# Grouped-query attention with a cache: six heads of the output weight moved to a second DMA queue, ring of eight slots instead of nine

## The chip, the cores and the metric

One core of a Trainium2 chip runs the program. The metric is the device time of one execution in microseconds (us). The kernel before was run three times: 388.24, 388.26 and 388.43 us, median 388.26 us.

The core has five instruction streams: PE (TensorE), DVE (VectorE), ACT (ScalarE), POOL (GpSimd) and SP (SyncE), and sixteen DMA engines that move data between device memory and the on-chip memory. In this kernel POOL and SP issue the transfers.

## The reference

```python
B, Sq, D = 32, 4, 1024
Hq, Hkv, Sk, Dh = 32, 4, 2048, 128
q = (x @ wq).reshape(B, Sq, Hq, Dh).transpose(0, 2, 1, 3)
k = jnp.repeat(k_cache, Hq // Hkv, axis=1)
v = jnp.repeat(v_cache, Hq // Hkv, axis=1)
scores = jnp.einsum("bhqd,bhkd->bhqk", q, k) * (Dh ** -0.5)
p = softmax(scores, axis=-1)
o = jnp.einsum("bhqk,bhkd->bhqd", p, v)
out = o.transpose(0, 2, 1, 3).reshape(B, Sq, Hq * Dh) @ wo
```

All inputs are bf16. For each of 32 batches the kernel reads 2 MB of keys and 2 MB of values; `wq` and `wo` are 8 MB each. That is about 151 MB in all, each byte used once.

## The kernel before

**The ring.** `slots` is a buffer of nine slots (`NSLOT`) of 8192 bf16 elements per partition, 2 MB each. All large inputs go through it in the order of the list `stream`: four loads of `wq`, then k of batches 0, 1 and 2, then v(0), k(3), v(1), k(4) and so on to k(31), v(29), v(30), v(31), and at last four loads of `wo`. Entry n uses slot n mod `NSLOT`. Each entry is four transfers of 512 KB with a semaphore for each; POOL issues them all, in order, at L144. Before entry n POOL waits until the work that reads entry n - `NSLOT` is done (`freed`): the last transposes of a k, the product `pv` of a v, the query projection for `wq`. For k and v a transfer is one group of heads; for `wo` it is a piece of two heads, two rows of 2 KB in each of 128 partitions. SP loads `x` at the start (L146) and stores the output at the end (L168); between these it has nothing to do.

**The work of a batch.** k arrives with positions on the partitions and is transposed on TensorE (`kt_fill`, L236, eight fills per batch into a ring of four PSUM banks), evacuated by DVE and ACT (L346, L348) into `KT_sb`. `qk` (L281) makes the scores of a batch in one PSUM tile; DVE takes the maximum (L372), ACT the exponential with its sum (L401), DVE the reciprocal and a diagonal matrix of it (L381, L382). `tr_fill` (L252) transposes the probabilities and scales them by that diagonal; `pv` (L263) multiplies with v; `ot_evac` (L361) copies the result into `oT_sb`. TensorE's order is written out: for batch i it runs `qk(i)`, `pv(i-1)`, the eight fills of k(i+2), and the four `tr_fill` of batch i.

**The output projection.** After `pv(31)` TensorE runs `oproj` (L314): 32 heads times two halves of 512 columns, 64 matmuls that accumulate in one PSUM tile, all of them reading `oT_sb` with the columns of all batches. They are queued in sixteen groups of four, each with a wait for its piece of `wo`. DVE and ACT then evacuate one half each (L391, L411), and SP stores the output.

`Program.emit` (L48) turns the named events into semaphore waits on each engine; an engine runs its list in order.

Of the kernel before, what the change touches and what calls it, by code (L numbers as in the profile page):

```python
# [8 lines left out]
BF16 = mybir.dt.bfloat16  # L9
# [45 lines left out]
def bass_standalone__gqa_block_cached__sampling_kernel(  # L55
# [8 lines left out]
    B, Sq, D = x.shape  # L64
    _, Hkv, Sk, Dh = k_cache.shape
    Hq = wq.shape[1] // Dh
# [5 lines left out]
    NKT = Sk // 128  # L72
    G = Hkv
    scale = float(Dh) ** -0.5
    NSLOT = 9
    SLOT = 8192
    NRING = 4
    KT_FILLS = 2 * G
    TR_FILLS = 4
    AHEAD = 2  # L80
    WQ_LOADS = 4
    WO_LOADS = 4
    HPL = Hq // WO_LOADS
    WO_PARTS = 4
    WO_PER = HPL // WO_PARTS

    x_flat = x.rearrange("b s d -> (b s) d")
    out_flat = out.rearrange("b s d -> (b s) d")
# [1 line left out]
    pr = Program()  # L90

    with ExitStack() as es:
        sb = lambda name, shape, dt: es.enter_context(nc.sbuf_tensor(name, shape, dt))
        slots = sb("slots", [128, NSLOT, SLOT], BF16)
        KT_sb = sb("KT_sb", [128, 2, G, Sk], BF16)
        QT_sb = sb("QT_sb", [128, B, Hq, Sq], BF16)
        oT_sb = sb("oT_sb", [128, Hq, NT], BF16)
# [18 lines left out]
        q_bank = ring_f32 + [ps_s[:, c * 512:(c + 1) * 512] for c in range(4)]  # L116

        pr.sems = {e: es.enter_context(nc.semaphore(f"s_{e}")) for e in Program.ENGINES}
        for n in ["x", "out"] + [f"slot{i}_{g}" for i in range(NSLOT) for g in range(G)] + [f"wo{i}" for i in range(WO_LOADS * WO_PARTS)]:
            pr.sems[n] = es.enter_context(nc.semaphore(f"s_{n}"))  # L120


# [3 lines left out]
        for b in range(B):  # L126
            stream.append(("v", b))
            if b + AHEAD + 1 < B:
                stream.append(("k", b + AHEAD + 1))
        stream += [("wo", i) for i in range(WO_LOADS)]  # L130
        slot_of = {l: n % NSLOT for n, l in enumerate(stream)}

        def freed(l):
            kind, i = l
            return {"wq": ("qproj", i), "k": ("kt", i, KT_FILLS - 1), "v": ("pv", i)}[kind]

        def slot(l):
            return slots[:, slot_of[l], :]

        wq_v = wq.rearrange("(p a k) n -> p a (k n)", a=WQ_LOADS, k=KT // WQ_LOADS)  # L140
        wo_v = wo.rearrange("(h p) n -> p h n", p=128)

        def fetch(dst, src):
            return lambda e: e.dma_start(dst, src, single_packet=True)  # L144
# [4 lines left out]
            out=ident[:], in_=ident[:], compare_op=ALU.not_equal, fill=1.0, base=0,  # L149
            pattern=[[-1, 128]], channel_multiplier=1), ["zero"], "ident")  # L150
        for n, l in enumerate(stream):
            kind, i = l
            waits = [freed(stream[n - NSLOT])] if n >= NSLOT else []
            s, v = f"slot{n % NSLOT}_", 16 * (n // NSLOT + 1)
            if kind == "wq":
                for q in range(G):
                    cols = slice(q * SLOT // G, (q + 1) * SLOT // G)
                    pr.load("pool", fetch(slot(l)[:, cols], wq_v[:, i, cols]), l + (q,), s + str(q), v, waits)
            elif kind in "kv":
                src = (k_cache if kind == "k" else v_cache)[i].rearrange("g (p t) d -> g p (t d)", p=128)  # L160
                for g in range(G):
                    pr.load("pool", fetch(slot(l)[:, g * NKT * Dh:(g + 1) * NKT * Dh], src[g]), l + (g,), s + str(g), v, waits)
            else:
                for q in range(WO_PARTS):
                    part = slot(l)[:, q * WO_PER * D:(q + 1) * WO_PER * D].rearrange("p (h n) -> p h n", n=D)
                    h0 = i * HPL + q * WO_PER
                    pr.load("pool", fetch(part, wo_v[:, h0:h0 + WO_PER, :]), ("wo", i, q), f"wo{i * WO_PARTS + q}", 16, waits)
        pr.op("sp", lambda e: e.dma_start(out_flat[:, :], out_sb).then_inc(pr.sems["out"], 16), ["out0", "out1"])  # L168
        pr.op("sp", lambda e: e.wait_ge(pr.sems["out"], 16))

# [135 lines left out]
                tr_fill(i, f)  # L306
        pv(B - 1)

        def oproj(i, h0, n):
            def fn(e):  # L310
                w = slot(("wo", i)).rearrange("p (h n) -> p h n", n=D)
                for h in range(h0, h0 + n):
                    for c in range(2):
                        ins = e.matmul(  # L314
                            ps_s[:, c * 512:(c + 1) * 512],
                            lhsT=oT_sb[:, h, :],
                            rhs=w[:, h - i * HPL, c * 512:(c + 1) * 512],
                            start=(h == 0),
                            stop=(h == Hq - 1),
                        )  # L320
                return ins

            return fn

        for i in range(WO_LOADS):
            for q in range(WO_PARTS):
                pr.op("pe", oproj(i, i * HPL + q * WO_PER, WO_PER),
                      [("wo", i, q), ("ot", B - 1), ("exp", B - 1)],
                      "oproj" if (i, q) == (WO_LOADS - 1, WO_PARTS - 1) else None)


        def evac(job):
# [131 lines left out]
```

## Time and profile before

| | |
|---|---|
| median of three runs | 388.26 us (388.24 to 388.43) |
| profiled execution: span | 386.1 us |
| profiled execution: its own time | not recorded beside the span; the median lies 2.2 us above the span |
| moved by DMA | 152.30 MB, mean 394 GB/s over the span |
| busy share of PE, DVE, ACT, POOL | 76%, 64%, 51%, 40% |
| k and v transfers, issue to landing (median) | 41.4 and 42.2 us |
| x transfer, issue to landing | 2.6 us |
| output transfer, issue to landing | 2.0 us |

How to read it: the span goes from the first to the last instruction of one profiled execution. The queue table names the queues: q0 is the ring (issued by POOL), q1 is SP's queue, q8 and q14 fetch the engines' instructions. DMA share is the mean busy share of the sixteen DMA engines in a stretch; the GB/s are what they moved in it. In the timeline a line gives start, length, engine, line of the kernel, operation, the tiles written and read, and in brackets the idle time before it and what ended that. PEclk is the part of TensorE's full clock that was granted. The chain of work that ended last goes back from the last instruction, at each step to what released it. The trace also records when each transfer raised its semaphore; it does so sixteen times, and the last of these is its landing.

### The profile page before, as it was taken

What the parts mean: (1) busy time and instruction counts of PE and PEld (TensorE: products, weight loads), DVE (VectorE), ACT (ScalarE), POOL (GpSimd) and SP (SyncE); (2) the same over time, 40 slices, a digit from 0 to 9 for tenths busy, and PEclk for the clock granted to TensorE, in tenths of its full rate; (3) what the DMA queues carried; (4) which work ended last, traced back from release to release, by engine and by line L of the source; (5) the groups of instructions that cost most, each with busy time, mean ns of one, the idle gap of its engine ahead of it and who ended that gap; (6) DMA issues with size and microseconds to landing.
All of it is one profiled execution on the core that took longest, in us unless ns stands there. A gap on an engine that the chain in (4) does not pass through costs nothing.

```text
span 386.1 us, 12016 instructions
## 1 busy us (share of the span) xinstructions
PE 293.4 (76%) x5446; PEld 238.9 (62%) x5448; DVE 245.3 (64%) x390; ACT 198.6 (51%) x230; POOL 154.1 (40%) x294
## 2 busy tenths in 40 slices
PE   1969777878887877677978877787868778776596
PEld 0968556666766666465866766666756666664542
DVE  0017887777676777677677777686767766774400
ACT  1016666655564666456656455466564666654300
POOL 8975344433344443344443334443334436500000
PEclk9999999999898999999899899898989999997689
DMA  7999999999999999999999999999999999999982
GB/s 276 413 407 407 407 407 407 409 408 407 407 410 407 409 408 407 405 409 406 408 409 404 410 407 410 407 411 407 406 408 408 409 408 406 410 407 404 389 322 112
DMA packets 41810, 152.30 MB, mean 394 GB/s; under 512 B 4640, under 2 KB 4640, under 8 KB 41760
## 3 DMA queue, kind: packets, MB, share of 16 engines
q0 software_dynamic: 41472, 151.01, 98.5%
q8 instruction: 43, 0.70, 0.8%
q1 hardware_dynamic: 288, 0.52, 0.5%
q14 instruction: 7, 0.06, 0.0%
HBM read 151.26 MB, written 0.26 MB: 392 GB/s over the span
## 4 chain that ended last, share of the span: by engine, by line
DMA 83%; PE 7%; POOL 5%; ACT 2%; issue 1%; POOLq 0%; DVE 0%
DMA slots<-in_k_cache_dram 45%; DMA slots<-in_v_cache_dram 23%; DMA slots<-in_wo_dram 11%; POOL slots L144 5%; DMA slots<-in_wq_dram 4%; ACT KT_sb L348 2%; PE ps_o L263 2%; PE ps_c L236 1%; PE ps_o L236 1%; PE ps_a L236 1%; PE ps_s L281 1%; PE ps_s L211 0%; PE ps_b L236 0%; PE ps_s L314 0%; PE ps_o L252 0%
## 5 line engine op out<-in xcount | busy, mean ns | idle before, releaser
L401 ACT ACTIVATE pp_sb<-ps_s,negmx 128x2048 bf16<-128x2048 f32 x32 | 62.9, 1967 | 93.0 <-DVE negmx L373 93.0
L144 POOL DMA_DIRECT2D slots<-in_k_cache_dram x128 | 66.8, 529 | 100.1 <-PE ps_o L263 93.1
L372 DVE TENSOR_REDUCE mx<-ps_s 128x1 f32<-128x2048 f32 x32 | 73.3, 2291 | 38.6 <-PE ps_s L281 38.6
L144 POOL DMA_DIRECT2D slots<-in_v_cache_dram x128 | 66.9, 529 | 75.3 <-PE ps_a L252 66.0
L263 PEld LDWEIGHTS ps_o<-pp_sb,slots 128*128 128x128 bf16 x2048 | 54.4, 97 | 53.6 <-issue 53.6
L263 PE MATMUL ps_o<-pp_sb,slots 128*128 128x32 bf16 x2048 | 56.9, 179 | 38.6 <-DMA slots<-in_v_cache_dram 37.6
L348 ACT ACTIVATE KT_sb<-ps_a 128x1024 bf16<-128x1024 bf16 x32 | 32.7, 1022 | 34.8 <-PE ps_a L236 34.7
L236 PE MATMUL ps_c<-ident,slots 128*128 128x128 bf16 x512 | 40.9, 224 | 7.5 <-DMA slots<-in_k_cache_dram 5.5
L346 DVE COPY KT_sb<-ps_b 128x1024 bf16<-128x1024 bf16 x64 | 43.6, 682 | 1.2 <-PE ps_b L236 0.8
L236 PE MATMUL ps_a<-ident,slots 128*128 128x128 bf16 x512 | 42.1, 229 | 2.0 <-DVE KT_sb L346 1.4
L236 PE MATMUL ps_b<-ident,slots 128*128 128x128 bf16 x512 | 41.8, 228 | 0.0
L236 PE MATMUL ps_o<-ident,slots 128*128 128x128 bf16 x512 | 40.2, 222 | 2.0 <-DVE KT_sb L346 1.0
L236 PEld LDWEIGHTS ps_c<-ident,slots 128*128 128x128 bf16 x512 | 31.7, 101 | 11.1 <-DMA slots<-in_k_cache_dram 9.8
L348 ACT ACTIVATE KT_sb<-ps_c 128x1024 bf16<-128x1024 bf16 x32 | 32.7, 1022 | 8.4 <-PE ps_c L236 8.4
L236 PEld LDWEIGHTS ps_a<-ident,slots 128*128 128x128 bf16 x512 | 31.7, 102 | 6.0 <-DMA slots<-in_k_cache_dram 3.0
L236 PEld LDWEIGHTS ps_o<-ident,slots 128*128 128x128 bf16 x512 | 31.7, 99 | 4.4 <-DVE KT_sb L346 3.1
L281 PE MATMUL ps_s<-KT_sb,QT_sb 128*32 128x512 bf16 x512 | 34.3, 389 | 0.0
L236 PEld LDWEIGHTS ps_b<-ident,slots 128*128 128x128 bf16 x512 | 33.9, 103 | 0.1
L346 DVE CAST pp_sb<-ps_a 128x512 bf16<-128x512 f32 x32 | 22.1, 691 | 17.9 <-PE ps_a L252 17.9
L348 ACT ACTIVATE KT_sb<-ps_o 128x1024 bf16<-128x1024 bf16 x32 | 32.7, 1022 | 0.2 <-PE ps_o L236 0.2
L346 DVE COPY KT_sb<-ps_a 128x1024 bf16<-128x1024 bf16 x32 | 22.1, 690 | 7.9 <-PE ps_a L236 7.9
L252 PE MATMUL ps_o<-diag,pp_sb 128*128 128x128 bf16 x128 | 13.2, 227 | 15.3 <-ACT KT_sb L348 15.3
(50 smaller groups left out, 308.9 us busy)
## 6 DMA issues: line engine op xcount, KB each, us to landing
slots<-in_k_cache_dram POOLq DMA_DIRECT2D x128, 512.0 KB, 41.4
slots<-in_v_cache_dram POOLq DMA_DIRECT2D x128, 512.0 KB, 42.2
slots<-in_wq_dram POOLq DMA_DIRECT2D x16, 512.0 KB, 9.8
slots<-in_wo_dram POOLq DMA_DIRECT2D x16, 512.0 KB, 42.6
pp_sb<-in_x_dram SPq DMA_DIRECT2D x1, 256.0 KB, 2.6
out_dram<-pp_sb SPq DMA_DIRECT2D x1, 256.0 KB, 2.0
```

What stands on the lines that cost most here:

```text
L144: return lambda e: e.dma_start(dst, src, single_packet=True)
L236: ins = e.transpose(dst[:, q * 128:(q + 1) * 128], slot(("k", b))[:, (g * NKT + t) * Dh:(g * NKT + t + 1) * Dh], ident[:, :],)
L252: ins = e.matmul(dst[:, q * 128:(q + 1) * 128], lhsT=P_sb[:, t * 128:(t + 1) * 128], rhs=diag[:, b % 2, :], start=True, stop=True)
L263: ins = e.matmul(ps_o[:, 32 * g:32 * (g + 1)], lhsT=v[:, (g * NKT + t) * Dh:(g * NKT + t + 1) * Dh], rhs=PT_sb[:, t, 32 * g:32 * (g + 1)], ...
L281: ins = e.matmul(ps_s[32 * g:32 * (g + 1), c * 512:(c + 1) * 512], lhsT=QT_sb[:, i, REP * g:REP * (g + 1), :], rhs=KT_sb[:, i % 2, g, c * ...
L346: pr.op("dve", lambda e: e.tensor_copy(dst, src), w, ("evac",) + job)
L348: pr.op("act", lambda e: e.activation(dst, src, ACT.Copy), w, ("evac",) + job)
L372: pr.op("dve", lambda e, i=i: e.tensor_reduce(mx[:, i:i + 1], ps_s[:, :], AX.X, ALU.max), [("qk", i)], ("max", i))
L401: pr.op("act", lambda e, i=i: e.activation(P_sb, ps_s[:, :], ACT.Exp, bias=negmx[:, i:i + 1], scale=scale, accum_out=ssum[:, i:i + 1]), [( ...
```

## The change

Six of the 32 heads of `wo` (`HSIDE`, 1.5 MB) leave the ring. They get a buffer of their own, `side` (12 KB per partition), and SP loads them right after `x` in sixteen transfers, without a wait. Transfer m takes eight partitions, four apart (m = 0: partitions 0, 4, ... 28), and in each the six rows of 2 KB. All sixteen raise one semaphore, `side`; the projection waits for its full count of 256.

The ring has eight slots instead of nine. `wo` is in it with 26 heads, that is thirteen pieces of two heads: three loads of four pieces and one load of one.

The projection starts with the six heads of `side` in one group of twelve matmuls, then goes through the thirteen pieces. Number and order of the matmuls stay as they were, by heads from 0 to 31.

```diff
-    NSLOT = 9
+    NSLOT = 8
...
-    WO_LOADS = 4
-    HPL = Hq // WO_LOADS
+    HSIDE = 6
+    WO_PER = 2
     WO_PARTS = 4
-    WO_PER = HPL // WO_PARTS
+    HPL = WO_PER * WO_PARTS
+    WO_PIECES = (Hq - HSIDE) // WO_PER
+    WO_LOADS = -(-WO_PIECES // WO_PARTS)
...
+        side = sb("side", [128, HSIDE, D], BF16)
...
-                for q in range(WO_PARTS):
+                for q in range(min(WO_PARTS, WO_PIECES - i * WO_PARTS)):
                     part = slot(l)[:, q * WO_PER * D:(q + 1) * WO_PER * D].rearrange("p (h n) -> p h n", n=D)
-                    h0 = i * HPL + q * WO_PER
+                    h0 = HSIDE + i * HPL + q * WO_PER
                     pr.load("pool", fetch(part, wo_v[:, h0:h0 + WO_PER, :]), ("wo", i, q), f"wo{i * WO_PARTS + q}", 16, waits)
+        for m in range(16):
+            p0 = 32 * (m // 4) + m % 4
+            pr.load("sp", lambda e, p0=p0: e.dma_start(side[p0:p0 + 29:4, :, :], wo_v[p0:p0 + 29:4, 0:HSIDE, :]),
+                    ("side", m), "side", 16 * 16)
...
-        for i in range(WO_LOADS):
-            for q in range(WO_PARTS):
-                pr.op("pe", oproj(i, i * HPL + q * WO_PER, WO_PER),
-                      [("wo", i, q), ("ot", B - 1), ("exp", B - 1)],
-                      "oproj" if (i, q) == (WO_LOADS - 1, WO_PARTS - 1) else None)
+        pr.op("pe", oproj(side, 0, HSIDE), [("side", 15), ("ot", B - 1), ("exp", B - 1)])
+        for n in range(WO_PIECES):
+            i, q = divmod(n, WO_PARTS)
+            w = slot(("wo", i))[:, q * WO_PER * D:(q + 1) * WO_PER * D].rearrange("p (h n) -> p h n", n=D)
+            pr.op("pe", oproj(w, HSIDE + n * WO_PER, WO_PER), [("wo", i, q)], "oproj" if n == WO_PIECES - 1 else None)
```

More of the change, by code (lines that the diff above doesn't have):

```diff
@@ L118, in bass_standalone__gqa_block_cached__sampling_kernel @@
         pr.sems = {e: es.enter_context(nc.semaphore(f"s_{e}")) for e in Program.ENGINES}
-        for n in ["x", "out"] + [f"slot{i}_{g}" for i in range(NSLOT) for g in range(G)] + [f"wo{i}" for i in range(WO_LOADS * WO_PARTS)]:
+        for n in ["x", "out"] + [f"slot{i}_{g}" for i in range(NSLOT) for g in range(G)] + [f"wo{i}" for i in range(WO_PIECES)] + ["side"]:
             pr.sems[n] = es.enter_context(nc.semaphore(f"s_{n}"))
@@ L307, in bass_standalone__gqa_block_cached__sampling_kernel, with oproj @@
         pv(B - 1)
-        def oproj(i, h0, n):
+        def oproj(w, h0, n):
             def fn(e):
-                w = slot(("wo", i)).rearrange("p (h n) -> p h n", n=D)
                 for h in range(h0, h0 + n):
@@ L316, in fn @@
                             lhsT=oT_sb[:, h, :],
-                            rhs=w[:, h - i * HPL, c * 512:(c + 1) * 512],
+                            rhs=w[:, h - h0, c * 512:(c + 1) * 512],
                             start=(h == 0),
```

## The prediction

> **What bounds the kernel now.** I read the page first: the queue table and the chain of work that ended last.
>
> ```profile
> q0 software_dynamic: 41472, 151.01, 98.5%
> q8 instruction: 43, 0.70, 0.8%
> q1 hardware_dynamic: 288, 0.52, 0.5%
> q14 instruction: 7, 0.06, 0.0%
> ...
> DMA 83%; PE 7%; POOL 5%; ACT 2%; issue 1%; POOLq 0%; DVE 0%
> ```
>
> The ring's transfers (q0) fill 98.5% of the sixteen DMA engines' time, and 83% of the chain is transfers. The change moves bytes from q0 to q1 and adds none, so the average says "no change". The end must therefore be read by itself. Here is the windows view (length, busy of PE, PEld, DVE, ACT, POOL, granted clock, DMA share, GB/s) at the start and in the last stage:
>
> ```profile
> 2.00:3.00 1.00, 0.00 (x0) 0.00 (x0) 0.00 (x0) 0.03 (x1) 1.00 (x3) 1.00 0.74 227
> 3.00:4.00 1.00, 0.61 (x6) 0.61 (x7) 0.00 (x0) 0.00 (x0) 1.00 (x3) 1.00 0.69 115
> 4.00:5.00 1.00, 0.46 (x5) 0.21 (x2) 0.50 (x1) 0.00 (x0) 1.00 (x3) 1.00 0.98 360
> ...
> 370.00:372.00 2.00, 2.00 (x11) 0.94 (x10) 0.00 (x0) 0.00 (x0) 0.00 (x0) 1.00 1.04 389
> 372.00:374.00 2.00, 2.00 (x11) 0.90 (x10) 0.00 (x0) 0.00 (x0) 0.00 (x0) 1.00 0.72 279
> 374.00:376.00 2.00, 2.00 (x11) 0.88 (x9) 0.00 (x0) 0.00 (x0) 0.00 (x0) 1.00 0.55 219
> 376.00:378.00 2.00, 2.00 (x11) 0.92 (x10) 0.00 (x0) 0.00 (x0) 0.00 (x0) 1.00 0.52 205
> 378.00:380.00 2.00, 1.95 (x10) 0.94 (x10) 0.00 (x0) 0.00 (x0) 0.00 (x0) 1.00 0.49 197
> ```
>
> From 372 us on, half of the DMA engines are done; the other half works on until about 380 us. The trace's landing records say since when: each transfer raises its semaphore sixteen times, once per engine. For a piece of wq that lands at 14.89 us the sixteen lie within 0.6 us; for the last piece of k31, counted from its first, they come at 0.0, 0.0, 0.2, 0.2, 0.2, 1.3, 1.6, 2.9 and then 6.4 to 8.4 us, the last at 344.38. So eight engines are early and eight late. The reason is q8: 43 fetches of TensorE's code, 16 KB each, go round eight engines, and each step in the records is some 1.5 us. The seven small fetches of q14 explain the 1.3, 1.6 and 2.9: three of the early eight are not quite early.
>
> Then the timeline, at the last k load and at the output projection:
>
> ```profile
> 344.42 0.45 PEld L236 LDWEIGHTS ps_c<-ident,slots 128*128 128x128 bf16 x8 [0.40 <-DMA slots<-in_k_cache_dram]
> ...
> 355.50 1.90 PE L281 MATMUL ps_s<-KT_sb,QT_sb 128*32 128x512 bf16 x16
> ...
> 365.30 1.87 PE L263 MATMUL ps_o<-pp_sb,slots 128*128 128x32 bf16 x64 [0.78 <-ACT pp_sb L348]
> ...
> 368.02 13.59 PE L314 MATMUL ps_s<-slots,oT_sb 128*128 128x512 bf16 x58 [0.85 <-DVE oT_sb L361]
> ...
> 381.84 0.55 PEld L314 LDWEIGHTS ps_s<-slots,oT_sb 128*128 128x128 bf16 x4 [0.73 <-DMA slots<-in_wo_dram]
> ```
>
> k31's third part starts the moment it lands. From there to the projection (368.02) nothing on the chain waits for a transfer: v31 has landed at 360.65, 4.65 us before pv(31) uses it. The 64 projection matmuls start 0.216 us apart. Piece 14 starts at once (380.57); piece 15 starts at 381.85, where the matmul before it (381.23) would have let it start at 381.45. That is the whole wait for wo: 0.40 us. The end hangs on two clocks that almost agree: k31's landing plus compute, and wo's last landing. Only 0.40 us can be had from wo.
>
> **Part by part.** The base is the profiled span, 386.1 us; the runs' median of 388.26 lies 2.2 us above it, and I carry that over unchanged.
>
> *Three wo pieces fewer at the end* (13 instead of 16). Pieces come 1.28 us apart, so wo's last landing is some 3.8 us earlier against k31's. The projection then waits for nothing and is TensorE-bound: -0.40 us. It cannot give more, since 64 matmuls at 0.216 us (13.8 us) stand behind the attention tail as before.
>
> *Nine slots become eight.* One slot is 2 MB, 5.1 us at 408 GB/s. A k load now takes 41.4 us from issue to landing (median), of which nearly all is queueing; one slot less leaves about 36 us queued, and an engine that is 8 us ahead of the others still has 28. Slot waits on POOL change their releaser (v31 waits for pv(26), which ends near 321 us, some 39 us before v31 is due), not the transfers. The last load of wo waits for pv(28), which ends near 341 us, and is used some 40 us later. Cost 0; if queueing fell to zero somewhere it would show as a DMA share under 0.95.
>
> *Sixteen transfers on SP.* They stand behind x, whose issue took 0.37 us and whose data came from 1.75 to about 2.9 us; nobody but the output transfer follows on SP, 380 us later. x keeps its place, so TensorE's first transposes are not moved. The wait on the side buffer sits at the projection and was fulfilled long before.
>
> *What they cost the ring.* The bytes must go through the same sixteen engines, ahead of most of the stream, and every k and v behind them lands later. How many engines? x's 128 rows made 144 packets: 128 of data, one a row, and 16 semaphore writes; the ring's packets are also one row each (4096 bytes, 128 a transfer). No row is seen split over engines, so a transfer of eight rows fills eight engines. The two ends are sixteen engines (48 packets of 2 KB on each) and eight (96 on each). I take eight, the nearer reading. A 2 KB packet of x took 84 ns: 96 x 84 = 8.06 us, and 16 semaphore writes of 9 ns add 0.14: 8.2 us on each of the eight (7.6 at the ring's spacing of 155 ns for 4 KB, 8.5 at the 87 ns that the output's packets took).
>
> *What the start hides.* In 2 to 5 us the engines moved 227, 115 and 360 GB/s where 408 would fit: (181 + 293 + 48) / 408 = 1.28 us unused. q1's packets can lie there, behind x; I take 0.9 of it (bounds 0 and 1.28). Net lag 7.3 us (6.3 to 8.5).
>
> *Which eight.* If they are the early ones, the slowest of these reaches 2.9 + 7.3 = 10.2 us at k31, against 8.4 for the late half: k31 lands 1.8 us later (0.8 to 3.0). The whole tail follows one for one, as nothing in it has slack before the projection. Sum: -0.40 + 1.8 = +1.4 us, 389.7 us (388.7 to 390.9). In words: the halves are levelled on average, but a landing is set by the worst engine, and the end was compute plus k31, not wo.
>
> [...]
>
> **Rivals.**
> 1. *The side load fits into the lead, and the tail is lighter* (faster). If its net lag is under 5.5 us (8.4 - 2.9), k31 lands as before and the 0.40 us is kept: 387.9. TensorE's granted clock was halved in much of 352 to 369 us: qk(31) took 1.90 us where qk(30) took 1.05, and the first three projection matmuls were 0.427 apart, not 0.216. A tail in other clock windows could save 0.85 + 0.63 more: 386.4. I price it at 387.1. For it: early engines with 8 us of lead. Against: 96 packets at 84 ns don't fit into 5.5 us unless most of the load lies in the start's gap.
> 2. *The eight engines are the late ones, or some of each.* Then the lag at k31 is 8.4 + 7.3: +7.3 - 0.40 = +6.9, 395.1 us. For it: no row ties q1 to a half. Against: q14's fetches all fell on the half that q8 leaves alone, so the halves are fixed sets and not mixed at random.
> 3. *It spreads over all sixteen.* 8.2 / 2 - 0.9 = 3.2 us on the late half too: +2.8, 391.1 us. Against it: rows are not split.
>
> **How the numbers follow.** Forecast 0.66, first rival 0.16, second 0.13, third 0.05. A measurement of this kernel can tell about 0.2% (0.78 us) from no change. Faster: most of rival one, 0.14. Same (387.5 to 389.0): the rest of it and the low end of the forecast, 0.19. Slower: 0.67. The range runs from rival one's price to past the third's, 387.1 to 391.6; outside lie the second rival and a little of the first.
>
> **What would show it.** Right: wo wait gone before the projection's last matmuls; landings of the wq loads up to 7 us later than before (26.1 us for the last) and k31's about 1.8 us later than 344.4; the DMA share at the end falling from 1.0 to near 0 in some 3 us instead of 8; all sixteen increments of a late transfer closer together. Wrong: k31 landing at or before 344.4 (rival one), near 351.7 with a half-busy end of longer than 8 us (rival two), or at 347.6 with the half-busy end of 8 us unchanged (rival three); or slot waits that leave the DMA share below 0.95 in the middle of the run, which would refute the eight-slot step.

## The result and the profile after

The changed kernel took 400.32 us (four runs, 399.00 to 401.78) against 388.35 us before (four runs): a ratio of 1.0307, 95% interval 1.0281 to 1.0334. The forecast was 389.7 us with a range up to 391.6. Its sign was right, its size was not: 12.0 us where 1.4 were expected. Even the dearest rival (395.1 us) fell short. The profiled execution took 401.78 us with a span of 400.0 us, 13.9 us above the span before.

The page of the changed kernel, queue table, chain of work that ended last and the SP queue's transfers:

```profile
q0 software_dynamic: 41040, 149.44, 95.0%
q1 hardware_dynamic: 1184, 2.10, 1.6%
q8 instruction: 43, 0.70, 0.7%
...
DMA 73%; PE 14%; POOL 5%; ACT 3%; DVE 2%; issue 1%; POOLq 0%
...
side<-in_wo_dram SPq DMA_DIRECT2D x16, 96.0 KB
```

q1 now has 1184 packets. x and the output make 288, so each of the sixteen transfers made 56: 48 rows of data and 8 semaphore writes. Eight engines take part in each, as the forecast read it. PE has twice its share of the chain (14% where the kernel before had 7%), because the end is now compute behind a load of the stream and no longer a transfer of wo.

The windows view of the changed kernel, columns as before (the last two are DMA share and GB/s), over the start and the last stage:

```profile
8.00:16.00 8.00, 2.84 (x28) 2.87 (x29) 0.00 (x0) 0.00 (x0) 8.00 (x17) 1.00 1.03 403
16.00:33.00 17.00, 8.41 (x111) 8.12 (x110) 0.00 (x0) 0.00 (x0) 6.70 (x13) 0.81 1.03 314
33.00:41.00 8.00, 7.85 (x109) 7.70 (x108) 1.72 (x3) 1.19 (x2) 2.09 (x4) 0.77 1.03 409
...
378.00:380.00 2.00, 1.42 (x54) 1.45 (x55) 0.10 (x1) 0.43 (x1) 0.00 (x0) 0.50 0.89 354
380.00:382.00 2.00, 1.52 (x20) 0.77 (x17) 0.29 (x1) 0.00 (x0) 0.00 (x0) 0.50 0.64 244
382.00:384.00 2.00, 2.00 (x6) 0.72 (x5) 0.00 (x0) 0.00 (x0) 0.00 (x0) 0.50 0.21 82
384.00:386.00 2.00, 2.00 (x9) 0.80 (x8) 0.00 (x0) 0.00 (x0) 0.00 (x0) 0.79 0.14 55
386.00:388.00 2.00, 2.00 (x11) 0.88 (x9) 0.00 (x0) 0.00 (x0) 0.00 (x0) 1.00 0.11 45
```

The kernel before, in the same stretch:

```profile
16.00:33.00 17.00, 13.88 (x246) 13.53 (x244) 5.32 (x9) 3.16 (x5) 12.95 (x25) 1.00 1.03 407
```

Two things were not there before. From 16 to 33 us the engines are fully busy (share 1.03) and yet move 314 GB/s instead of 407. In the packet records a 4 KB packet of the ring takes 159 ns (median) from 8 to 16 us and 215 ns from 17 to 33 us; a 2 KB packet of the side load takes 84 and then 111. The engines without side load are slowed too: their increments, 1.27 us apart from transfer to transfer at 14 us, come 1.7 us apart at 20 us. And the run-out has another form: the 8 us of half-busy engines are gone, but a share of 0.11 to 0.14, about two engines of sixteen, goes on to 388 us.

The landing records of k31's last piece say the same. Before, its sixteen increments came from 336.00 to 344.38 us. Now the first comes at 340.96, and counted from it: 0.0, 0.2, twelve between 7.3 and 11.4, 13.7 and 15.5, the last at 356.48. So k31 lands 12.10 us later: 4.96 us because even the earliest engine is late, 7.14 us because the spread grew from 8.38 to 15.52.

The timeline of the changed kernel, at the first and the seventh of the eight fills of k31 and at the projection:

```profile
353.41 0.77 PEld L243 LDWEIGHTS ps_a<-ident,slots 128*128 128x128 bf16 x8
...
357.99 0.49 PEld L243 LDWEIGHTS ps_c<-ident,slots 128*128 128x128 bf16 x8
...
380.92 4.66 PE L320 MATMUL ps_s<-side,oT_sb 128*128 128x512 bf16 x12 [0.47 <-DVE oT_sb L367]
...
385.42 11.39 PE L320 MATMUL ps_s<-slots,oT_sb 128*128 128x512 bf16 x52
```

The seventh fill is the one that needs k31's last piece. It starts at 357.99 us, 1.51 us after that landing and without a wait: TensorE was still busy with the fills before it, at a granted clock of 0.50 from 350.7 to 357.5 us. So in this execution the last load that the chain waited for was not k31 but v28, one place earlier in the stream: it landed at 351.37 us, 12.13 us later than before (339.24), and `pv(28)`, which needs it, started at 351.72 with k31's fills right behind. (The chain of work names DVE's `negmx` there, which ended at the same moment; `pv` does not wait for it.) The lag is the same as k31's, and I go on measuring at k31.

The wait for wo is gone: the 52 matmuls that read the ring run at 0.216 us apart without a gap. But the first nine starts after the projection's beginning are 0.38 to 0.43 us apart, since TensorE's granted clock was 0.50 from 374.6 to 384.8 us. In this execution the tail behind k31 became 1.8 us longer instead of 0.40 us shorter (13.93 us for the last matmul's start, 12.10 for k31). Before, such stretches of half clock had lain at 352.3 to 359.1 and 362.5 to 369.3 us; the four runs of the changed kernel spread over 2.8 us.

### The profile page after: what moved, and what is told of

Same layout as the page of the kernel before. It is cut to its first block, busy times and chain, and to the rows that moved or that the text cites. A ratio compares the mean times of both kernels' runs of the same rounds, so it can differ in the third digit from the quotient of the medians.

```text
span 400.0 us, 12031 instructions
## 1 busy us (share of the span) xinstructions
PE 301.8 (75%) x5448; PEld 246.8 (62%) x5448; DVE 245.6 (61%) x390; ACT 198.2 (50%) x230; POOL 152.0 (38%) x291
## 3 DMA queue, kind: packets, MB, share of 16 engines
q1 hardware_dynamic: 1184, 2.10, 1.6%
## 4 chain that ended last, share of the span: by engine, by line
DMA 73%; PE 14%; POOL 5%; ACT 3%; DVE 2%; issue 1%; POOLq 0%
DMA slots<-in_v_cache_dram 47%; DMA slots<-in_k_cache_dram 19%; DMA slots<-in_wq_dram 7%; POOL slots L147 5%; PE ps_s L320 4%; PE ps_o L270 3%; ACT KT_sb L354 2%; DVE mx L378 2%; PE ps_c L243 1%; PE ps_a L243 1%; ACT pp_sb L407 1%; PE ps_o L243 1%; PE ps_s L288 1%; PE ps_b L243 1%; PE ps_s L218 0%
## 5 line engine op out<-in xcount | busy, mean ns | idle before, releaser
L243 PE MATMUL ps_c<-ident,slots 128*128 128x128 bf16 x512 | 42.5, 230 | 5.3 <-DMA slots<-in_k_cache_dram 4.3
L243 PE MATMUL ps_a<-ident,slots 128*128 128x128 bf16 x512 | 43.3, 233 | 1.4 <-DVE KT_sb L352 1.4
L243 PE MATMUL ps_o<-ident,slots 128*128 128x128 bf16 x512 | 41.6, 227 | 2.3 <-DVE KT_sb L352 1.2
L243 PE MATMUL ps_b<-ident,slots 128*128 128x128 bf16 x512 | 42.9, 232 | 0.0
L243 PEld LDWEIGHTS ps_c<-ident,slots 128*128 128x128 bf16 x512 | 33.4, 104 | 9.2 <-DMA slots<-in_k_cache_dram 7.9
L243 PEld LDWEIGHTS ps_a<-ident,slots 128*128 128x128 bf16 x512 | 33.1, 105 | 4.8 <-issue 2.0
L243 PEld LDWEIGHTS ps_o<-ident,slots 128*128 128x128 bf16 x512 | 32.9, 102 | 4.3 <-DVE KT_sb L352 2.9
L243 PEld LDWEIGHTS ps_b<-ident,slots 128*128 128x128 bf16 x512 | 34.8, 105 | 0.1
```

The source lines that it names most:

```text
L243: ins = e.transpose(dst[:, q * 128:(q + 1) * 128], slot(("k", b))[:, (g * NKT + t) * Dh:(g * NKT + t + 1) * Dh], ident[:, :],)
```

## The experiments

Four theories were tried. **Two terms**: (a) the transfers to partitions 64 to 127, carried by the same eight engines as those to 0 to 63, slow every engine down; (b) two of these eight also take TensorE's code fetches, so their lags add. **Slots**: the ring of eight runs short while the query projection holds its slots. **Number**: sixteen small transfers cost by their number. **Bytes early**: 1.5 MB ahead of the stream cost this much on any engines.

**Eight slots alone.** The kernel before, one edit:

```diff
-    NSLOT = 9
+    NSLOT = 8
```

> The kernel before with eight slots and nothing else changed. The theory that the smaller ring costs nothing: 388.3 us (387.9 to 388.8), k and v 36 to 37 us from issue to landing, no stretch under 400 GB/s between 5 and 350 us. The rival that the ring of eight runs short while the query projection still holds its slots, and that this makes the slow stretch of the changed kernel (314 GB/s from 16 to 33 us): slower by 3 us or more, with a stretch near 310 GB/s before 40 us.

Measured: 388.60 us against 388.10, ratio 1.0009 (0.9999 to 1.0018). Its windows view:

```profile
16.00:33.00 17.00, 14.09 (x224) 13.95 (x222) 4.16 (x7) 2.39 (x4) 10.36 (x21) 0.90 1.03 409
```

The smaller ring costs at most 0.7 us (the interval's upper end); no slow stretch. The theory of the slots falls. POOL does wait in the changed kernel, up to 8.6 us for the query projection, but engines with a share of 1.03 were not waiting for work.

**The transfers in reversed order.**

```diff
-        for m in range(16):
+        for m in reversed(range(16)):
```

> The changed kernel with the sixteen side transfers issued in reversed order, those to partitions 64 to 127 first. Theory: the slow stretch belongs to the transfers into partitions 64 to 127, which the same eight engines carry. Then it moves: about 310 GB/s from some 4 us to some 21 us, 400 and more afterwards, first landings of k31 again some 5 us later than before, and the total stays at 400 us (398.5 to 402). Rival (the ring runs short of slots, or the eight engines' lag itself slows all): the slow stretch stays at 16 to 33 us.

Measured: 399.34 us (397.61 to 400.57), ratio 1.0284 (1.0248 to 1.0320).

```profile
6.00:18.00 12.00, 3.29 (x32) 3.32 (x33) 0.00 (x0) 0.00 (x0) 12.00 (x25) 1.00 1.03 312
22.00:41.00 19.00, 15.07 (x208) 14.81 (x209) 2.98 (x5) 2.39 (x4) 6.25 (x13) 0.82 1.03 408
```

The slow stretch moved to the front with the transfers to the upper partitions. In the packet records half of the 768 side packets have started by 19.1 us, and the rate is back at over 400 GB/s from 20 us on; in the changed kernel half have started by 16.6 us, and the rate falls in the window that begins at 17. k31's first increment came at 339.98, its spread was 15.6 us. The stretch belongs to one half of the transfers.

**The same rows into the lower partitions.** Eight transfers keep their source and get another destination (the zeroing of partitions 64 to 127 and the waits that go with it are not printed):

```diff
+            d0 = p0 % 64
+            into = side if m < 8 else junk      # junk: the key buffer, not yet in use
-            ... e.dma_start(side[p0:p0 + 29:4, :, :], wo_v[p0:p0 + 29:4, 0:HSIDE, :])
+            ... e.dma_start(into[d0:d0 + 29:4, :, :], wo_v[p0:p0 + 29:4, 0:HSIDE, :])
```

> The changed kernel; the eight transfers that went to partitions 64 to 127 read the same rows but write them to partitions 0 to 63 of the key buffer, before its first use; partitions 64 to 127 of the side buffer are set to zero by DVE, so this part of the projection is left out. Theory: with no writes into the upper partitions there is no slow stretch; the lag on the eight engines (7.6 us and more) and its meeting with the code fetches on two of them stay: k31's earliest increment at 336 to 337 us, its last at 351.5 to 352.5, total 395 us (393.8 to 396.5). Rival that the sources (rows of wo), the number of small transfers or the ring's slots make the slow stretch: it stays, total 400 us.

Measured: 395.58 us (395.56 to 396.43), ratio 1.0197 (1.0182 to 1.0212). Its windows view, in the slow stretch's place and at the end:

```profile
16.00:33.00 17.00, 10.98 (x147) 10.70 (x145) 0.00 (x0) 0.00 (x0) 6.70 (x13) 0.81 1.03 408
...
376.00:378.00 2.00, 2.00 (x6) 0.73 (x5) 0.00 (x0) 0.00 (x0) 0.00 (x0) 0.50 0.63 246
378.00:380.00 2.00, 2.00 (x10) 0.88 (x9) 0.00 (x0) 0.00 (x0) 0.00 (x0) 0.98 0.20 80
380.00:382.00 2.00, 2.00 (x11) 0.88 (x9) 0.00 (x0) 0.00 (x0) 0.00 (x0) 1.00 0.13 53
```

The slow stretch is gone with the destination alone: sources, sizes and number of transfers are the same. k31's first increment is at 337.25 (1.25 us later than before), its last at 351.99, and the run-out again ends with some two engines. What is left, 7.5 us, is for the most part term (b): of the 7.61 us by which k31's last increment is late, 6.36 are the wider spread (14.74 against 8.38). The 1.25 us of the earliest engine are something else, and the changed kernel has it too: from 4 to 16 us it moves 378 GB/s and this run 377, where the kernel before moved 410, though the median packets still take 159 and 84 ns. By an estimate from these rows, (410 - 377) x 12 / 408, that is 1.0 us. Its cause stays open.

**One wide transfer.**

```diff
-        for m in range(16): ...
+        pr.load("sp", lambda e: e.dma_start(side[:, :, :], wo_v[:, 0:HSIDE, :]), ("side", 15), "side", 16)
```

> The changed kernel with one transfer of 128 partitions for the side buffer in place of sixteen. Theory: 768 packets of data on sixteen engines (16 semaphore writes), each with 48 packets, 4.1 us, of which the start hides some 0.9: no slow stretch, the late half stays the late half, k31 lands 3.2 us later than before (347.6), the wait for wo (0.40 us) is gone, total 391.1 us (390.2 to 392.3). Rival that side bytes early are what costs, on whatever engines: 395 us or more.

Measured: 391.12 us (390.49 to 391.77), ratio 1.0077 (1.0060 to 1.0093).

```profile
16.00:33.00 17.00, 13.81 (x216) 13.52 (x214) 1.38 (x2) 0.86 (x2) 8.79 (x17) 1.00 1.03 409
```

k31 landed at 348.23 us, 3.85 later than before (3.23 of it on the first engine, the spread 9.0). The same bytes, as early, in one transfer over sixteen engines cost 3.0 us. So 9 of the 12 us come from how they were cut up, not from being early.

**Two heads instead of six.**

```diff
-    HSIDE = 6
+    HSIDE = 2
```

> The changed kernel with two heads in the side buffer instead of six: again sixteen transfers of eight partitions, each a third as large, and fifteen wo pieces in the ring. Theory, cost by bytes: the slow stretch costs a third of 5.0 us (1.7), the eight engines lag by 32 packets of 84 ns less what the start hides (some 2.5 us instead of 7.6), so the two of them that also fetch code end some 10.7 us behind the first; k31's last increment 3.5 to 4.5 us later than before (348 to 349), total 391 to 392.5 us. Rival, cost by the number of small transfers: 398 us or more.

Measured: 391.31 us (390.88 to 393.41), ratio 1.0090 (1.0061 to 1.0119).

```profile
10.00:12.00 2.00, 1.07 (x11) 1.10 (x12) 0.00 (x0) 0.00 (x0) 2.00 (x5) 1.00 1.04 417
12.00:18.00 6.00, 4.39 (x56) 4.21 (x53) 0.00 (x0) 0.00 (x0) 6.00 (x12) 1.00 1.04 329
18.00:24.00 6.00, 3.77 (x65) 3.66 (x66) 0.00 (x0) 0.00 (x0) 3.66 (x9) 1.00 1.03 406
```

As many transfers, a third of the bytes: the slow stretch is about 6 us instead of 17, k31's spread is 9.8 us and its last increment 3.78 us later than before (348.16). The cost goes with the bytes, and the theory of the number falls.

**Sixteen partitions to a transfer, eight apart and four apart.**

```diff
-        for m in range(16): ...
+        for m in range(8):      # rows m, m + 8, ... m + 120
+            pr.load("sp", lambda e, m=m: e.dma_start(side[m:m + 121:8, :, :], wo_v[m:m + 121:8, 0:HSIDE, :]), ("side", m), "side", 8 * 16)
```

The first eight rows of each transfer lie in partitions 0 to 63, its other eight in 64 to 127.

> The changed kernel with eight side transfers of sixteen partitions (m, m + 8, ... m + 120) in place of sixteen of eight. [...] If only the half counts, there is no slow stretch and the time is that of the single wide transfer, 391.1 us (390.3 to 392.3), k31's last increment near 348. [...]

The second one takes rows p0, p0 + 4, ... p0 + 60, with p0 = 64 * (m // 4) + m % 4.

> As the run before it, but each transfer's sixteen partitions are four apart, so that one transfer stays within partitions 0 to 63 or within 64 to 127 and half of its engines write into the other half. Theory: as many bytes cross as in the changed kernel (0.79 MB), so some 4 to 5 us are lost in a stretch under 350 GB/s while the side load runs, spread over all engines: 394.5 to 396.5 us, with k31's earliest increment 4 us later than in the step-8 run. Rival, that crossing is not the cause: the same time as the step-8 run.

Measured: 395.96 us (ratio 1.0193, 1.0173 to 1.0212) and 395.85 us (1.0201, 1.0171 to 1.0232). The windows view of the first and of the second:

```profile
8.00:18.00 10.00, 0.67 (x7) 0.70 (x8) 0.00 (x0) 0.00 (x0) 10.00 (x21) 1.00 1.04 306
```

```profile
8.00:18.00 10.00, 1.88 (x19) 1.91 (x20) 0.00 (x0) 0.00 (x0) 10.00 (x20) 1.00 1.04 310
```

Both are slow for as long as the side load runs, to about 20 us. In both the sixteen engines share the load evenly (k31's spread is 9.4 and 9.0 us), and k31's first increment is at 343.1 and 343.0 us: 7 us late, of which the wide transfer shows 3.2 for the bytes and so 3.9 for the cut. The step-8 run speaks against the narrower form of my theory, in which only the half of the partitions mattered and this cut was to cost no more than the wide transfer: it took 395.96 us against 391.12. The step-4 run was expected 4 us behind the step-8 run at k31's earliest increment; it came level, so its forecast held in the total only. Which engine writes into which half in these two cuts was an assumption: the traces have no engine numbers.

By these runs the rate holds with one transfer of 128 partitions (405 GB/s from 4 to 16 us) and, after the first microseconds, with transfers of eight rows, four apart, into partitions 0 to 63 (403 to 408 GB/s). It falls to 312 to 329 GB/s with the same eight rows into partitions 64 to 127, and to 306 and 310 GB/s with sixteen rows eight or four apart.

**Four partitions to a transfer, two heads.**

```diff
+        for m in range(32):
+            p0 = 16 * (m // 4) + m % 4
+            ... e.dma_start(side[p0:p0 + 13:4, :, :], wo_v[p0:p0 + 13:4, 0:HSIDE, :])
```

> The changed kernel with two heads in the side buffer, loaded in 32 transfers of four partitions, which should fill four engines with 64 packets each (5.4 us, some 4.9 net). It tells where the two engines are that take code fetches beside the side load. If they are among these four: k31's spread is 8.4 + 4.9 = 13.3 us. If they are not: the spread stays at 8 to 9 us, and the four engines show lags of 5 to 8 us without steps from code fetches. [...] Total 390 to 392 us in the second case, 395 us or more in the first.

Measured: 391.72 us (390.42 to 392.83), ratio 1.0089 (1.0060 to 1.0118).

```profile
8.00:10.00 2.00, 0.00 (x0) 0.00 (x0) 0.00 (x0) 0.00 (x0) 2.00 (x5) 1.00 1.04 390
10.00:12.00 2.00, 0.70 (x8) 0.73 (x9) 0.00 (x0) 0.00 (x0) 2.00 (x5) 1.00 1.01 308
12.00:14.00 2.00, 2.00 (x21) 2.00 (x20) 0.00 (x0) 0.00 (x0) 2.00 (x5) 1.00 1.03 406
14.00:16.00 2.00, 2.00 (x39) 2.00 (x37) 0.00 (x0) 0.00 (x0) 2.00 (x5) 1.00 1.06 356
16.00:18.00 2.00, 0.28 (x6) 0.11 (x2) 0.00 (x0) 0.00 (x0) 2.00 (x4) 1.00 0.99 309
...
28.00:30.00 2.00, 1.54 (x15) 1.57 (x16) 0.00 (x0) 0.00 (x0) 0.00 (x0) 0.50 1.02 334
30.00:32.00 2.00, 2.00 (x22) 2.00 (x20) 0.00 (x0) 0.00 (x0) 0.00 (x0) 0.50 1.03 412
```

After the side load four engines lag by 5.5 to 5.8 us, and at 130 us they stand at 5.8 to 6.6, where engines with code fetches have gained two steps of 1.5 us. k31's spread is 8.7 us, close to the 8.4 before. So no engine of these four takes TensorE's fetches, and the side load's lag hides behind theirs. That is what the forecast assumed for all eight. If these four are among the eight that the changed kernel used, the two engines on which the lags add are among the other four.

What this run lost, 3.33 us on k31's first increment, is for the most part the slow stretch, more than the 1.7 us that the half alone would cost by an estimate (a third of the changed kernel's 4.96 us for a third of its bytes). Within it the rate came back once, and the packet records say when. Four transfers cover sixteen rows in 32 packets. Counted in order of start, rows 0 to 15 begin at 2.9 us, rows 16 to 31 at 8.5, rows 32 to 47 at 11.6, rows 48 to 63 at 14.2, and the last packet at 29.3. The rate is 387 to 392 GB/s from 4 to 10 us, 308 from 10 to 12, 406 from 12 to 14, and then at most 356 until 30 us. So, about 1 us behind the packets at most, rows 0 to 15 and 32 to 47 are fast and the six other groups slow, rows 16 to 31 too, although they lie in the lower half. Rows 0 to 15 and 32 to 47 are just the ones that stand in the first four places of the changed kernel's fast transfers 0 to 7. So in these runs the rate goes with a row's partition together with its place in its transfer, and not with the half. That a row's place stands for its engine is a reading that no trace here shows.

**The last load of wo in single heads.** The kernel before; nothing early is moved.

```diff
+                per = 1 if i == WO_LOADS - 1 else WO_PER
-                for q in range(WO_PARTS):
+                for q in range(HPL // per):
```

> The kernel before, with the last load of wo cut into eight pieces of one head instead of four of two; nothing early is moved. It prices the term of the prediction that only 0.40 us can be had from wo: after the last landing two projection matmuls remain instead of four. Theory: 0.2 to 0.4 us faster (387.7 to 387.9 beside 388.1), at the limit of what can be told. Rival, that wo's end holds the kernel by more (the half-busy DMA engines of the last 8 us): 1 us or more faster.

Measured: 387.87 us against 388.11, ratio 0.9993 (0.9984 to 1.0002). A gain of 0.24 us cannot be told from none, but one of 1 us can be excluded. The half-busy engines at the end of the kernel before were no reserve: once wo's wait of 0.40 us is gone, the compute behind k31 is the limit. No kernel in this study is measurably faster than the one before.

## Why the prediction was wrong

**The reading of the end held, with one correction.** A late load of the stream plus compute sets the end, and wo's wait is worth 0.40 us: the wait vanished in every variant, and the single heads bounded its worth (a gain of 0.6 us at most). In six of the nine experiments' profiles the fill that needs k31's last piece starts 0.04 us after its landing, as before; in the changed kernel and the three others a stretch of half clock delays it by 0.43 to 1.51 us, so there the tail did not follow k31 "one for one". And the row at 344.42 us in the prediction belongs to the last of k31's four pieces (landed at 344.38), not to its third (343.08); nothing hangs on that.

**Eight slots cost 0**: held, 0.5 us with an interval from -0.04 to 0.7.

**Eight engines, 8.2 us, net 7.3**: held. The packet count shows eight engines, and between 40 and 60 us, with the slow stretch over, the eight lag the others by 7.5 to 8.8 us. That SP issued a transfer every 0.72 us, twice what x took, did not matter. The estimate of the start's gap was near enough: the wide transfer, priced at 391.1 in the third rival, took 391.12.

**Which eight: failed.** The forecast took the early eight, because code fetches of q8 and q14 fell on different halves, and judged that the halves were fixed sets which SP's transfers would not mix. They mix. In the changed kernel's records the eight engines without side load start level; six of them climb in steps to 7.3 to 7.9 us, two stay at 0.0 and 0.2. Of the eight with side load, which stand at 7.6 to 8.7 us at 45 us, two climb too, in steps of some 1.5 us, to 13.7 and 15.5. So six of the fetching engines lie outside SP's eight and two inside, and a landing waits for the worst. The second rival had this ("or some of each"), with k31 near 351.7 and 395.1 us; with the slow stretch taken away the kernel has 351.99 and 395.58. That it agrees so closely is in part luck: the spread grew by 6.36 us and not by 7.3, and 1.25 us at the start, which the rival did not have, made up for it. It stood at 0.13, far too low: nothing in the trace before ties a queue to engines, and two independent sets of eight out of sixteen seldom are disjoint.

**What no step contained** was the slow stretch, worth 3.7 us at k31's first increment (340.96 against 337.25 in the lower-half run) and 4.7 us in time (400.32 to 395.58). The step "What they cost the ring" took each packet at its duration in the trace before, 84 ns for 2 KB, with 155 ns for 4 KB as a bound, and so held that bytes only queue behind one another; in the stretch a 2 KB packet took 111 ns and a 4 KB packet 215, on engines with and without side load. So k31's 12.10 us, where the forecast had 1.8, are 3.7 of the slow stretch, 7.1 of the wider spread and 1.25 at the start. The bound of 155 ns came from rows in which every transfer had 128 partitions, and the range inherited it. With six heads in the side buffer the slow stretches ran at 306 to 314 GB/s in place of 403 to 409; where the packets meet is not shown by any run here.

**The tail's clock** was named as a chance in the first rival and went the other way, 1.8 us longer from k31's landing in the profiled execution.

## What to carry to other kernels

When a transfer is cut into pieces of few partitions, ask which engines carry each piece and into which partitions it writes, and measure the GB/s while it runs: here eight-row pieces into partitions 64 to 127 took the whole core from 407 to 314 GB/s for 17 us, and the same rows into partitions 0 to 63 left it at 408. Read the sixteen increments of a landing, not only the mean DMA share: a load is ready with its slowest engine (before, the fill that needs k31's last piece started 0.04 us after the last of them, 8.42 us after the first), and an extra load on some engines left the landing's spread alone only where it missed those that were already late (8.7 us with four engines, 15.5 with eight). The half-idle stage at the end was no reserve, because without wo's wait, 0.40 us, compute is the limit.

## What the hardware showed

- The fetches of q8 (43 of 16 KB, read as TensorE's code, since TensorE has 10,894 of the 12,016 instructions) went round eight DMA engines, each time with a step of some 1.5 us, and put each of the eight 6.4 to 8.4 us behind within 340 us. In this kernel, bound by transfers, that is the whole 8.4 us between the first and the last increment of k31, though the queue table shows 0.8%.
- Side writes of 2 KB rows took the whole core from 407 to 314 GB/s with eight rows a transfer into partitions 64 to 127, and to 306 and 310 GB/s with sixteen rows a transfer, while the mean busy share stayed at 1.03 to 1.04. Share without GB/s does not show it.
- An eight-partition transfer of 96 KB held SP for 0.68 us in most cases, a 128-partition transfer of 256 KB for 0.38 us.
